# Free scatters, another quarter order, and a tile's evacuation split in two in a chunked attention and two-layer MoE kernel

## The chip, the core and the metric

One Trainium2 chip, one of its cores. Five engines work from queues of their own, each in order: TensorE (PE, with PEld for weight loads), VectorE (DVE), ScalarE (ACT), GpSimd (POOL) and SyncE (SP, which here only issues DMAs). The metric is the device time of one execution in microseconds; lower is better.

## The reference

Three stages, one behind the other, on float32 inputs:

```python
# 1. attention in chunks of 64 positions, batch 8, heads 8, sequence 576, head size 64
scores = scale * matmul(q_c, k_c.T);  scores -= max(scores)
attn = exp(scores);  attn = attn / (sum(attn) + 1e-09)
x = matmul(attn, v_c)                       # reshaped to 4608 tokens x 512
# 2. dense layer, 512 -> 2048 -> 512
h = maximum(x @ w_in, 0);  x = (h * h) @ w_out
# 3. top-1 of 8 experts, 512 -> 1024 -> 512
logits = x @ w_gate + modality_bias[modality_id]
e_idx = argmax(logits);  gate_w = softmax(logits)[e_idx]
for e in range(8):                          # the tokens whose expert is e
    out[mask] = gate_w[mask] * (maximum(x[mask] @ w1[e], 0) @ w2[e])
```

## The kernel before

**Tiles and blocks.** The 4608 tokens are 36 tiles of 128, worked on in 9 blocks of 4 tiles, counted from 0. Numbers are split into a high and a low float16 half, and a GEMM runs three passes over them.

**The dense layer of a block.** Blocks 0 to 2 compute x @ w_in plainly (`mm1`, matmul at L792). Blocks 3 to 8 use 28 products of a Strassen-like scheme (`prod`, 12 matmuls each, L621), which write four PSUM banks (two named hh, two oo); `after` brings partial results out, scaled by `al`, a factor that hangs on the largest norm in the block. `x_norm` computes that norm with a small matmul `np` (L726) and a reduction on VectorE (L728). `square` squares the hidden values into a high half (ScalarE) and a low half (GpSimd, L663). The second GEMM, `mm2` (L810), takes the four tiles one behind the other; a tile is four quarters of 12 matmuls, a quarter is four of the 16 values of f (the slices of 128 hidden units), and tile t accumulates in bank t of the four.

**The chain of a tile behind mm2.** `x2_evac` squares and sums the result on ScalarE, forms a power-of-two scale on VectorE, and writes the high and low half `xs`. `x2_tr` has SyncE transpose `xs` by DMA into `x2t` (L830) and store it to DRAM as x2d (L831). `route_a` multiplies by the gate weights (`lp`, L838) and picks the expert on VectorE (L841 to L853). `route_b` ranks the tokens of an expert (`rp`, L858 and L859). `route_c` and `route_d` scatter token and gate weight into the DRAM table `meta` by GpSimd (L884). lp, rp and np share one PSUM buffer, `ps_r`.

**Experts.** The sorted tokens are worked on in pairs of tiles, 256 tokens each. For a pair, SyncE transposes the gathered rows (L1126), 7 products give the hidden layer (L1199), 7 more the output (L1267), and `put` scatters it to `out` (L1293). SyncE and ScalarE also issue the loads of expert weights from the DRAM copy wsp (`load_part` L1075, `early_w` L1086). The products of pair 0 (`first1`) are laid between the last two tiles' mm2, those of pair 1 follow.

**What sets the order.** The program order is written by a loop over `steps` at the end: TensorE's big pieces (`mm1`, `prod`, `mm2`, `first1`) at planned times T, and before each of them `flush`, which takes from a heap the events that are due: the attention of later tiles (`attn_events`: scores, PV products `xp`, `x_tsplit`, `x_norm`), the chain of a tile, and weight work. `COST` gives what an event loads on ScalarE and VectorE; an event that finds the engine full is put off. `need` lists what must have been issued before a piece; while it is missing, flush goes on with a later time. So what is issued there stands ahead of the piece on TensorE's queue.

```python
need += [(x2_evac, b0 - 4 + t) for t in range(4)]                                   # L1642, prod
need = [(square, su, f, a[1] % 2) for f in range(0, 4 * a[2] + 4, 2)] + ...         # L1646, mm2
for t, qq in M2 if su == 0 else [(t, qq) for t in range(nt) for qq in range(4)]:    # L1570
```

Of the kernel before, what the change touches and what calls it, by code (L numbers as in the profile page):

```python
# [28 lines left out]
EW = 0.8  # L29
READY = 2  # L30
# [3 lines left out]
def kernel(  # L34
# [778 lines left out]
    def x2_evac(i):  # L813
        j = where[i][2]
# [9 lines left out]
        a["xs"], a["ui"] = xs, ui  # L824
# [57 lines left out]
    def route_d(i):  # L882
        a = x2.pop(i)
        nc.gpsimd.indirect_dma_start(  # L884
            out=meta[:, :], out_offset=bass.IndirectOffsetOnAxis(ap=a["di"][:, 0:1].bitcast(U32), axis=0),
            in_=a["mt"], in_offset=None,
        )

    mp = {}
# [17 lines left out]
    def meta_gather(n, name):  # L907
        ri = mp["ri" + name]
        if name == "a":
            mg = pp_b[0][:n]  # L910
        else:
            mg = xtall[:n, 7168:8192].bitcast(F32)
        nc.gpsimd.indirect_dma_start(
            out=mg, out_offset=None, in_=meta.rearrange("(t r) c -> t (r c)", r=PAIR),
            in_offset=bass.IndirectOffsetOnAxis(ap=ri[:n, 0:1].bitcast(U32), axis=0),
        )
        mp["mg" + name] = mg
# [244 lines left out]
    def once(fn, *a):  # L1162
        if a[-1] < PAIRS and (fn, *a) not in gone and a[-1] in pair:
            gone.add((fn, *a))
            fn(*a)

# [124 lines left out]

    def put(t, o):
        nc.gpsimd.indirect_dma_start(  # L1293
            out=out[:, :], out_offset=bass.IndirectOffsetOnAxis(ap=t.bitcast(U32), axis=0),
            in_=o, in_offset=None, bounds_check=NT - 1, oob_is_err=False,
        )

# [5 lines left out]
        x_norm: (0.0, 0.2), x2_evac: (1.2, 1.1), route_a: (0.0, 0.9),  # L1303
# [29 lines left out]
    def flush(t, n=None, room=None, dt=None):  # L1333
# [9 lines left out]
        while ev and ev[0][0] <= t or due:  # L1343
# [27 lines left out]
            if room is not None:  # L1371
# [3 lines left out]
                if full and t - at_ < SLACK and fn not in (w_form, w_split):  # L1375
# [19 lines left out]
    def attn_events(i, a0):  # L1395
# [6 lines left out]
                (43.5, x_t34, 0), (46.0, x_norm, 0), (48.0, x_tsplit, 0),  # L1402
# [154 lines left out]
    for su, (b0, nt, sb) in enumerate(supers):  # L1557
# [12 lines left out]
        for t, qq in M2 if su == 0 else [(t, qq) for t in range(nt) for qq in range(4)]:  # L1570
# [14 lines left out]
            d = (4.0, 11.0, 16.0, 19.0, 25.0) if i < NTILE - 2 and i != SEEN - 1 else (4.0, 11.0, 16.0, 19.0, 21.0) if i < NTILE - 1 and i != SEEN - 1 else (4.0, 11.0, 16.0, 19.0, 19.2) if i < NTILE - 1 else (4.0, 8.2, 12.0, 14.0, 14.5)  # L1585
            ch = [(T, x2_evac, (i,)), (T + d[0], x2_tr, (i,)), (T + d[1], route_a, (i,)), (T + d[2], route_b, (i,)), (T + d[3], route_c, (i,)), (T + d[4], route_d, (i,))]
# [38 lines left out]
    with tc.manual_schedule():  # L1625
# [3 lines left out]
        for n, (T, fn, a) in enumerate(steps):  # L1629
# [5 lines left out]
            if fn is mm1:  # L1635
                need = [(attn_x, subs[su][0] + t) for t in range(4)]
                need += [(x2_evac, a[1])] if su == PLANNED and a[1] < 2 else []
            elif fn is prod:
# [3 lines left out]
                need += [(x2_evac, b0 - 4 + t) for t in range(4)]  # L1642
            elif fn is first1:
                need = [(x2_evac, NTILE - 4), (x2_evac, NTILE - 3)][:1 + (a[0] > 0)]
            elif su >= HALVED:
                need = [(square, su, f, a[1] % 2) for f in range(0, 4 * a[2] + 4, 2)] + [(square, su, KF - 2, 0)] * (a[1] > 0)  # L1646
            elif su:
                need = [(x2_evac, supers[su][0] + a[1] - 2)]
# [151 lines left out]
```

## Time and profile before

| what | value |
|---|---|
| median of 3 runs | 1266.74 us (1266.11 to 1266.81) |
| the profiled execution's own time | 1266.4 us |
| its span | 1264.7 us |
| TensorE busy, share of the span | 1173.8 us, 93% |
| VectorE | 917.6 us, 73% |
| ScalarE | 706.6 us, 56% |
| GpSimd | 690.6 us, 55% |
| granted TensorE clock, mean | 0.978 |

The profiled execution is the one whose rows are read; its own time is longer than the span by 1.7 us, which lies around the first and last instruction. The product stretches of blocks 3 to 8 begin at 328, 416, 511.9, 604.7, 705.5 and 792 us of the span, the experts run alone from 901 us on. Busy shares are means over the span; a single stretch can look quite different, and an engine's idle time costs something only where another waits for it.

### The profile page before, as it was taken

The numbers are of one execution on the slowest core, as the hardware profiler recorded it, in microseconds if no ns is written. First come the engines' busy times: TensorE is split into PE (matmuls) and PEld (weight loads), VectorE is DVE, ScalarE is ACT, GpSimd is POOL, SyncE is SP. The second block draws the span as 40 slices with busy tenths as digits, with TensorE's granted clock in tenths as the row PEclk, the third lists the DMA queues.
The fourth block names the chain that finished last, engine by engine and source line by source line (L and its number), as shares of the span: only waits on it lengthen the run. The fifth ranks groups of instructions, "written<-read, shape, count | busy, mean of one in ns | idle before, by whom it ended". The sixth has DMA issues, their size and how long they took to land. (4 is left out here: it accounts for less than half of the span.)

```text
span 1264.7 us, 33052 instructions
## 1 busy us (share of the span) xinstructions
PE 1173.8 (93%) x12910; PEld 833.9 (66%) x12910; DVE 917.6 (73%) x2031; ACT 706.6 (56%) x1392; POOL 690.6 (55%) x641
## 2 busy tenths in 40 slices
PE   5898999999999989899989799999579999999996
PEld 4443444444774754664855664856579999999995
DVE  6899785675696895696886894854577766776663
ACT  6887583574574574574664573633335555555552
POOL 4488374587584484474574483555144455455442
PEclk9899999999899999999999899999799999999998
DMA  9455524324425537436526444255714445733241
GB/s 375 161 161 140 119 53 80 72 51 104 102 44 151 116 80 160 103 82 159 131 70 151 96 72 122 51 186 105 146 44 97 101 93 167 212 93 88 73 102 52
DMA packets 189208, 144.46 MB, mean 114 GB/s; under 512 B 126634, under 2 KB 163534, under 8 KB 187874
## 3 DMA queue, kind: packets, MB, share of 16 engines
q1 hardware_dynamic: 180386, 117.91, 38.8%
q0 software_dynamic: 7632, 20.54, 5.3%
q10 hardware_dynamic: 1008, 3.67, 1.2%
q8 instruction: 103, 1.69, 0.6%
q14 instruction: 79, 0.65, 0.2%
HBM read 204.06 MB, written 34.48 MB: 189 GB/s over the span
## 5 line engine op out<-in xcount | busy, mean ns | idle before, releaser
L810 PEld LDWEIGHTS <-big 128*128 128x128 f16 x1728 | 164.6, 98 | 203.4 <-POOL big L663 9.1
L810 PE MATMUL oo<-big,big 128*128 128x512 f16 x1056 | 237.7, 381 | 3.4 <-POOL big L772 3.4
L1199 PEld LDWEIGHTS <-big 128*128 128x128 f16 x3192 | 192.3, 99 | 20.1 <-issue 16.0
L810 PE MATMUL hh<-big,big 128*128 128x512 f16 x672 | 150.1, 379 | 6.4 <-POOL big L663 6.1
L792 PE MATMUL hh<-xtall,big 128*128 128x512 f16 x576 | 129.3, 382 | 0.1
L1199 PE MATMUL hh<-big,big 128*128 128x128 f16 x2040 | 129.0, 220 | 0.0
L621 PEld LDWEIGHTS <-big 128*128 128x128 f16 x1152 | 112.5, 99 | 22.4 <-issue 7.4
L489 POOL TENSOR_TENSOR ee<-ee,rc 128x512 f32<-128x512 f32 x36 | 39.9, 1108 | 125.1 <-DVE rc L487 71.0
L117 DVE SCALAR_TENSOR_TENSOR stage<-raw,stage 128x256 f16<-128x256 f32 x112 | 73.6, 660 | 41.9 <-ACT stage L114 36.7
L792 PEld LDWEIGHTS <-big 128*128 128x128 f16 x576 | 55.1, 98 | 64.1 <-issue 2.0
L1267 PEld LDWEIGHTS <-xtall 128*128 128x128 f16 x840 | 79.5, 98 | 11.2 <-issue 3.1
L1293 POOL DMA_INDIRECT out_dram<-raw,tib x30 | 35.5, 1183 | 90.7 <-DVE raw L117 79.2
L311 POOL TENSOR_TENSOR raw<-raw 128x256 f32<-128x256 f32 x64 | 52.7, 823 | 55.8 <-DVE stage L117 23.8
L114 ACT ACTIVATE stage<-raw 128x256 f16<-128x256 f32 x112 | 45.3, 410 | 62.3 <-DMA wsp<-stage 35.6
L772 POOL TENSOR_TENSOR big<-sn,big 128x512 f16<-128x512 f32 x48 | 59.4, 1242 | 32.4 <-DVE sn L117 16.1
L1267 PE MATMUL oo<-big,xtall 128*128 128x256 f16 x600 | 73.5, 273 | 2.7 <-DVE raw L117 2.7
L663 POOL TENSOR_TENSOR big<-r,big 128x512 f16<-128x512 f32 x48 | 61.6, 1295 | 26.1 <-ACT big L114 24.1
L663 POOL TENSOR_TENSOR big<-sn,big 128x512 f16<-128x512 f32 x48 | 61.8, 1299 | 24.0 <-ACT big L114 23.9
L114 ACT ACTIVATE big<-hh 128x512 f32<-128x512 f32 x62 | 36.9, 595 | 64.1 <-PE hh L1199 50.9
L1160 POOL TENSOR_TENSOR big<-big 128x512 f16<-128x512 f32 x34 | 39.5, 1181 | 49.6 <-ACT big L114 49.6
L117 DVE SCALAR_TENSOR_TENSOR qkt<-qk,qkt 128x1024 f16<-128x1024 f32 x32 | 47.2, 1475 | 17.3 <-ACT qkt L114 16.8
L884 POOL DMA_INDIRECT meta<-mt,di x36 | 42.2, 1172 | 22.5 <-issue 10.2
(384 smaller groups left out, 2690.3 us busy)
## 6 DMA issues: line engine op xcount, KB each, us to landing
big<-wsp SPq DMA_DIRECT2D x111, 1024.0 KB
big<-wsp SPq DMA_DIRECT2D x37, 512.0 KB
qk<-in_qk_dram SPq DMA_DIRECT2D x34, 512.0 KB
wsp<-stage SPq DMA_DIRECT2D x224, 64.0 KB
x2d<-xs SPq DMA_DIRECT2D x36, 256.0 KB
vv<-in_v_dram SPq DMA_DIRECT2D x34, 256.0 KB
big<-in_w_in_dram SPq DMA_DIRECT2D x16, 512.0 KB
raw<-in_w_out_dram SPq DMA_DIRECT2D x16, 512.0 KB
```

Of the source, the lines that this page charges most:

```text
L114: nc.scalar.activation(out=out, in_=in_, func=func, **kw)
L117: nc.vector.scalar_tensor_tensor(out=out, in0=in0, scalar=s, in1=in1, op0=op0, op1=op1, **kw)
L311: nc.gpsimd.tensor_tensor(out=quad(out_), in0=quad(in0), in1=quad(in1), op=op)
L489: eng.tensor_tensor(out=ee, in0=ee, in1=rc.unsqueeze(2).to_broadcast([128, H, 64]), op=ALU.mult)
L621: nc.tensor.matmul(ps[:, f * 256:f * 256 + 256], lhsT=block(k, la, kk, 2 * n + f), rhs=xa(lb, kk), start=k in (1, 5, 2, 4) and f + m + kk ...
L663: nc.gpsimd.tensor_tensor(out=lo, in0=c, in1=hi, op=ALU.subtract)
L772: nc.gpsimd.tensor_tensor(out=lo, in0=q32.rearrange("p (f n) -> p f n", f=nf), in1=hi, op=ALU.subtract)
L792: nc.tensor.matmul(hp[:, q_ * n:(q_ + 1) * n], lhsT=wi[:, la, kk, f * 128:f * 128 + 128], rhs=x[:, lb, kk, :], start=i == 0, stop=i == 3 * ...
L810: nc.tensor.matmul(ps, lhsT=g[:, la, f, c:c + 128], rhs=wo[:, lb, f, :], start=f == 0 and n == 0, stop=f == KF - 1 and n == 2)
L884: nc.gpsimd.indirect_dma_start(out=meta[:, :], out_offset=bass.IndirectOffsetOnAxis(ap=a["di"][:, 0:1].bitcast(U32), axis=0), in_=a["mt"], ...
L1199: nc.tensor.matmul(ps[:, f * 128:f * 128 + 128], lhsT=WB[0][:, n, la, kk, f * 128:f * 128 + 128], rhs=xa(lb, kk), start=first and f + m + ...
L1267: nc.tensor.matmul(ps, lhsT=hb[:, la, f * 128:f * 128 + 128], rhs=WB[1][:, n, lb, f, :], start=first and f + m == 0, stop=True, skip_group ...
```

## The change

**Scatters.** The scatters to `out` (`put`) and to `meta` (`route_d`) are declared free of each other (`free_of`), since each writes rows of its own; the gather of `meta` gets a dependency on every scatter ahead of it.

**Quarter order.** In blocks 3 to 8, tile 0 takes its mm2 quarters in the order 0, 2, 1, 3, and a quarter asks only for the squares of its own four f, where before it asked for those of all quarters up to it.

**Evacuation in two events.** `x2_evac` keeps the square, the sum and the scale; the new `x2_scale`, due XS = 1.5 us later, writes the two halves and `ui`. Both have a COST of their own, and neither is put off because an engine is full. The later steps of the chain are planned at 11.5, 18, 21 and 26 us behind mm2 instead of 11, 16, 19 and 25.

**Banks one by one.** A block's first four products (n = 0, k = 1, 5, 2, 4), which start the four banks, each ask for `x2_scale` of the one tile that holds their bank, where before every product asked for the evacuation of all four. In `attn_events`, x_norm is due at 54.0 instead of 46.0, behind x_tsplit.

**Pair 0.** Its products now also ask for x_sum of pair 0.

```diff
-        s, isv = scale_bits(ss, [128, 1], "ts")
+        a["xs"], a["sc"] = xs, scale_bits(ss, [128, 1], "ts")
+    def x2_scale(i):
+        j = where[i][2]
+        a = x2[i]
+        xs, (s, isv) = a["xs"], a["sc"]
         act(xs[:, 0], a["ps"], scale=s[:, 0:1])
         stt(xs[:, 1], a["ps"], s[:, 0:1], xs[:, 0], ALU.mult, ALU.subtract)
...
     def route_d(i):
-        nc.gpsimd.indirect_dma_start(
+        ins = nc.gpsimd.indirect_dma_start(
...
+        free_of(ins, "meta")
+        scattered.append(ins)
...
+        for x in scattered:
+            tc.add_manual_dep(ins.ins, x.ins.name, mybir.DependencyInfo(mybir.DependencyClass.Sync, mybir.DependencyReason.DATA))
...
+    def free_of(ins, group):
+        tc.declare_no_dep(ins.ins, group=group, reason="rows of their own")
+        tc.add_to_no_dep_group(group, ins.ins)
...
     def put(t, o):
+        free_of(ins, "out")
...
-        x_norm: (0.0, 0.2), x2_evac: (1.2, 1.1), route_a: (0.0, 0.9),
+        x_norm: (0.0, 0.2), x2_evac: (0.7, 0.4), x2_scale: (0.6, 0.8), route_a: (0.0, 0.9),
...
-                if full and t - at_ < SLACK and fn not in (w_form, w_split):
+                if full and t - at_ < SLACK and fn not in (w_form, w_split, x2_evac, x2_scale):
...
-                (43.5, x_t34, 0), (46.0, x_norm, 0), (48.0, x_tsplit, 0),
+                (43.5, x_t34, 0), (48.0, x_tsplit, 0), (54.0, x_norm, 0),
...
-        for t, qq in M2 if su == 0 else [(t, qq) for t in range(nt) for qq in range(4)]:
+        for t, qq in M2 if su == 0 else [(t, qq) for t in range(nt) for qq in ((0, 2, 1, 3) if su >= HALVED and t == 0 else range(4))]:
...
-            ch = [(T, x2_evac, (i,)), (T + d[0], x2_tr, (i,)), (T + d[1], route_a, (i,)), ...
+            ch = [(T, x2_evac, (i,)), (T + XS, x2_scale, (i,)), (T + d[0], x2_tr, (i,)), (T + d[1], route_a, (i,)), ...
...
-                need += [(x2_evac, b0 - 4 + t) for t in range(4)]
+                need += [(x2_scale, b0 - 4 + (1, 5, 2, 4).index(a[2]))] if a[1] == 0 and a[2] in (1, 5, 2, 4) else []
             elif fn is first1:
-                need = [(x2_evac, NTILE - 4), (x2_evac, NTILE - 3)][:1 + (a[0] > 0)]
+                need = [(x_sum, 0)] + [(x2_scale, NTILE - 4), (x2_scale, NTILE - 3)][:1 + (a[0] > 0)]
             elif su >= HALVED:
-                need = [(square, su, f, a[1] % 2) for f in range(0, 4 * a[2] + 4, 2)] + [(square, su, KF - 2, 0)] * (a[1] > 0)
+                need = [(square, su, f, a[1] % 2) for f in range(4 * a[2], 4 * a[2] + 4, 2)] + [(square, su, KF - 2, 0)] * (a[1] > 0)
```

**Where instructions move.** First TensorE's queue at the seam of blocks 6 and 7 (701 us in the trace before), from the last matmuls of mm2 (oo_117 is its fourth bank) to the first product of block 7, which writes hh_114; lp and rp are routing matmuls, xp is PV, np the norm. Before:

```order
L810 MATMUL oo_117<-big_88,big_89 128x512
...
L838 MATMUL lp<-wgs,x2t 128x16
...
L858 MATMUL rp<-run,ones_h 128x8
...
L859 MATMUL rp<-oh,tri_h 128x8
...
L538 MATMUL xp<-pt_105,vs_99 64x64
...
L838 MATMUL lp<-wgs,x2t 128x16
...
L621 MATMUL hh_114<-xtall,big_87 128x256
```

After (lines after L811 are those of the changed file):

```order
L539 MATMUL xp<-pt_105,vs_99 64x64
...
L727 MATMUL np<-xn_8996,ones_f 128x4
...
L811 MATMUL oo_117<-big_88,big_89 128x512
...
L622 MATMUL hh_114<-xtall,big_87 128x256
...
L622 MATMUL oo_117<-raw,big_87 128x256
```

The two lp groups, the rp pair and xp no longer stand between mm2 and the first product: xp and np stand ahead of mm2's last quarter, and routing comes later, between products.

The same place at the seam of blocks 2 and 3 (324 us before), changed kernel only:

```order
L811 MATMUL oo_117<-big_88,big_89 128x512
...
L539 MATMUL xp<-pt_105,vs_99 64x64
...
L727 MATMUL np<-xn_3314,ones_f 128x4
...
L863 MATMUL rp<-run,ones_h 128x8
...
L864 MATMUL rp<-oh,tri_h 128x8
...
L622 MATMUL hh_114<-xtall,big_87 128x256
```

Here np and the rp pair moved to the place directly ahead of the first product, and the two lp groups that stood there before are gone from it.

Second, SyncE's queue at the first pairs (from 874.88 us in the trace before), from the two transposes of pair 2 (big_89) over two weight loads (big_87) to the transpose and store of the last tile; names in brackets are the semaphores that a row waits for, and DMAHW0 to DMAHW7 are the slots that the loads and transposes of SyncE and ScalarE use in turn. Before:

```order
L1126 DMA_TRANSPOSE big_89<-big_89 128x8x128 [waits DMASW6_49,DMAHW3_49,PE_49,Pool_49]
L1126 DMA_TRANSPOSE big_89<-big_89 128x8x128 [waits DMASW7_49,PE_49,Pool_49]
...
L1075 DMA big_87<-wsp 128x2048 [waits DMAHW3_49,PE_49]
...
L1075 DMA big_87<-wsp 128x4096 [waits DMAHW4_49,PE_49]
L830 DMA_TRANSPOSE x2t<-xs 128x8x128 [waits DMAHW7_49,DMAHW6_49,DVE_49]
L831 DMA x2d<-xs 128x1024 [waits DMAHW7_49]
```

After:

```order
L1136 DMA_TRANSPOSE big_89<-big_89 128x8x128 [waits DMASW6_49,DMAHW3_49,PE_49,Pool_49]
L1136 DMA_TRANSPOSE big_89<-big_89 128x8x128 [waits DMASW7_49,DMAHW5_49,PE_49,Pool_49]
...
L1085 DMA big_87<-wsp 128x2048 [waits DMAHW3_49,PE_49]
...
L1085 DMA big_87<-wsp 128x4096 [waits DMAHW5_49,PE_49]
L835 DMA_TRANSPOSE x2t<-xs 128x8x128 [waits DMAHW7_49,DMAHW6_49,DVE_49]
L836 DMA x2d<-xs 128x1024 [waits DMAHW7_49]
```

The rows keep their order, but the second weight load now waits for slot DMAHW5 instead of DMAHW4. On ScalarE's queue at the same place, the last weight load of pair 0 (big_88) stands among the evacuations. Before:

```order
L1086 DMA big_88<-wsp 128x2048 [waits DMAHW2_49]
L114 ACTIVATE xs,ss<-oo_117 128x512 [waits DMAHW5_49,PE_49]
L114 ACTIVATE xs<-oo_117,tss 128x512 [waits DVE_49]
L114 ACTIVATE big_87<-hh_115 128x512 [waits PE_49]
L114 ACTIVATE xtall<-pt_106 128x512
...
L1086 DMA big_88<-wsp 128x2048 [waits DMAHW5_49]
L114 ACTIVATE big_87<-hh_114 128x512 [waits PE_49]
```

After:

```order
L1096 DMA big_88<-wsp 128x2048 [waits DMAHW2_49]
L115 ACTIVATE xs,ss<-oo_117 128x512 [waits PE_49]
L115 ACTIVATE big_87<-hh_115 128x512 [waits PE_49]
L115 ACTIVATE xtall<-pt_106 128x512 [waits DVE_49]
...
L1096 DMA big_88<-wsp 128x2048 [waits DMAHW4_49]
L115 ACTIVATE big_87<-hh_114 128x512 [waits PE_49]
L115 ACTIVATE ex,se<-lg,nm 128x8
L115 ACTIVATE xs<-oo_117,tss 128x512 [waits DVE_49]
```

The load asks for DMAHW4 instead of DMAHW5, and the second half of the evacuation (xs<-oo_117,tss) has moved behind it.

## Rows read from the trace of the kernel before

**Rows 1.** The page: busy time by engine; GpSimd's square group (busy, mean ns).
```profile
PE 1173.8 (93%) x12910; PEld 833.9 (66%) x12910; DVE 917.6 (73%) x2031; ACT 706.6 (56%) x1392; POOL 690.6 (55%) x641
...
L663 POOL TENSOR_TENSOR big<-r,big 128x512 f16<-128x512 f32 x48 | 61.6, 1295 | 26.1 <-ACT big L114 24.1
```

**Rows 2.** TensorE's waits: what waited for what, us, times, longest.
```profile
PE hh L1199 <- ACT big L114: 12.2, 1, 12.2
...
PE hh L810 <- POOL big L663: 6.1, 4, 2.6
PE oo L621 <- ACT r L114: 5.4, 5, 2.6
PE hh L621 <- ACT sn L114: 5.1, 4, 1.9
PE rp L858 <- DVE lg L117: 5.0, 2, 4.4
...
PE xp L538 <- DVE vs L117: 2.6, 3, 1.9
...
PE xp L538 <- ACT vs L114: 2.0, 2, 1.1
...
PE rp L859 <- DVE oh L117: 1.5, 2, 0.7
```

**Rows 3.** Busy by stretch: us, PE, PEld, DVE, ACT, POOL, clock, DMA, GB/s.
```profile
328.00:370.00 42.00, 42.00 (x509) 36.41 (x504) 36.06 (x80) 28.04 (x55) 29.03 (x27) 0.94 0.37 86
...
416.00:460.30 44.30, 41.19 (x551) 35.83 (x550) 39.41 (x88) 29.29 (x60) 26.82 (x25) 1.00 0.46 102
...
511.90:558.00 46.10, 42.30 (x528) 36.33 (x528) 37.77 (x85) 30.10 (x61) 27.98 (x26) 0.96 0.39 90
...
604.70:650.70 46.00, 41.36 (x552) 35.87 (x551) 41.23 (x91) 30.75 (x63) 25.36 (x23) 1.00 0.41 103
...
705.50:748.70 43.20, 40.57 (x452) 35.28 (x450) 40.78 (x81) 28.10 (x56) 30.29 (x28) 0.97 0.46 78
```

**Rows 4.** Timeline of TensorE, VectorE, ScalarE at 701 us: start, us, [idle before <-releaser].
```profile
701.36 0.18 PE L858 MATMUL rp<-run,ones_h 128*128 128x8 f16 x1 [4.39 <-DVE lg L117]
...
700.82 0.22 DVE L117 SCALAR_TENSOR_TENSOR lg<-lp,ui,bias_t 128x8 f32<-128x8 f32 x1
...
702.77 0.15 DVE L117 SCALAR_TENSOR_TENSOR run<-run,oh 128x8 f16<-128x8 f16 x1
...
704.22 1.23 DVE L117 SCALAR_TENSOR_TENSOR qkt<-qk,qkt 128x1024 f16<-128x1024 f32 x1 [0.26 <-ACT qkt L114]
...
706.96 0.75 DVE L117 SCALAR_TENSOR_TENSOR xs<-oo,tss,xs 128x512 f16<-128x512 f32 x1 [0.69 <-ACT xs L114]
...
703.15 1.04 ACT L114 ACTIVATE qkt<-qk 128x1024 f16<-128x1024 f32 x1
```

**Rows 5.** Timeline of the pair seam: SyncE's x2t issues, TensorE's lp, ScalarE's wait.
```profile
852.27 1.29 SPq L830 DMA_TRANSPOSE x2t<-xs  x1
...
888.10 8.69 SPq L830 DMA_TRANSPOSE x2t<-xs  x1
...
855.41 0.36 PE L838 MATMUL lp<-wgs,x2t 128*128 128x16 f16 x8
...
907.80 0.35 PE L838 MATMUL lp<-wgs,x2t 128*128 128x16 f16 x8
...
900.73 0.60 ACT L114 ACTIVATE big<-hh 128x512 f32<-128x512 f32 x1 [12.88 <-DMA big<-big]
```

**Rows 6.** Timeline of the end: VectorE's last results and GpSimd's scatters.
```profile
1250.54 0.48 DVE L117 SCALAR_TENSOR_TENSOR raw<-xq,fsb,ms 128x256 f32<-128x256 f32 x1 [2.93 <-ACT ms L114]
...
1255.78 0.88 DVE L117 SCALAR_TENSOR_TENSOR raw<-oo,fsb,ms 128x256 f32<-128x256 f32 x2 [2.12 <-PE oo L1267]
...
1251.50 1.00 POOL L1293 DMA_INDIRECT out_dram<-raw,tib  x1 [5.13 <-DVE raw L117]
...
1259.31 0.98 POOL L1293 DMA_INDIRECT out_dram<-raw,tib  x1 [3.29 <-DMA out_dram<-raw,tib]
```

More of the change, by code (lines that the diff above doesn't have):

```diff
@@ L29 @@
 EW = 0.8
+XS = 1.5
 READY = 2
@@ L813, in x2_evac @@
     def x2_evac(i):
-        j = where[i][2]
         a = x2[i]
@@ L823, in x2_evac @@
         stt(ui, isv, 1.0, blk[j]["u"], ALU.mult, ALU.mult)
-        a["xs"], a["ui"] = xs, ui
+        a["ui"] = ui
     def x2_tr(i):
@@ L887, in route_d @@
         )
+        free_of(ins, "meta")
+        scattered.append(ins)
+    scattered = []
     mp = {}
@@ L912, in meta_gather @@
             mg = xtall[:n, 7168:8192].bitcast(F32)
-        nc.gpsimd.indirect_dma_start(
+        ins = nc.gpsimd.indirect_dma_start(
             out=mg, out_offset=None, in_=meta.rearrange("(t r) c -> t (r c)", r=PAIR),
@@ L1165, in once @@
             fn(*a)
+            done.add((fn, *a))
     def banks(x, p=0):
@@ L1290, in pair_o @@
             put(t2, o2)
+    def free_of(ins, group):
+        tc.declare_no_dep(ins.ins, group=group, reason="rows of their own")
+        tc.add_to_no_dep_group(group, ins.ins)
     def put(t, o):
-        nc.gpsimd.indirect_dma_start(
+        ins = nc.gpsimd.indirect_dma_start(
             out=out[:, :], out_offset=bass.IndirectOffsetOnAxis(ap=t.bitcast(U32), axis=0),
@@ L1584 @@
                 continue
-            d = (4.0, 11.0, 16.0, 19.0, 25.0) if i < NTILE - 2 and i != SEEN - 1 else (4.0, 11.0, 16.0, 19.0, 21.0) if i < NTILE - 1 and i != SEEN - 1 else (4.0, 11.0, 16.0, 19.0, 19.2) if i < NTILE - 1 else (4.0, 8.2, 12.0, 14.0, 14.5)
-            ch = [(T, x2_evac, (i,)), (T + d[0], x2_tr, (i,)), (T + d[1], route_a, (i,)), (T + d[2], route_b, (i,)), (T + d[3], route_c, (i,)), (T + d[4], route_d, (i,))]
+            d = (4.0, 11.5, 18.0, 21.0, 26.0) if i < NTILE - 2 and i != SEEN - 1 else (4.0, 11.0, 16.0, 19.0, 21.0) if i < NTILE - 1 and i != SEEN - 1 else (4.0, 11.0, 16.0, 19.0, 19.2) if i < NTILE - 1 else (4.0, 8.2, 12.0, 14.0, 14.5)
+            ch = [(T, x2_evac, (i,)), (T + XS, x2_scale, (i,)), (T + d[0], x2_tr, (i,)), (T + d[1], route_a, (i,)), (T + d[2], route_b, (i,)), (T + d[3], route_c, (i,)), (T + d[4], route_d, (i,))]
             if i == 3:
@@ L1636 @@
                 need = [(attn_x, subs[su][0] + t) for t in range(4)]
-                need += [(x2_evac, a[1])] if su == PLANNED and a[1] < 2 else []
+                need += [(x2_scale, a[1])] if su == PLANNED and a[1] < 2 else []
             elif fn is prod:
@@ L1641 @@
                 need += [(w_split, a[1], m) for m in range(4)]
-                need += [(x2_evac, b0 - 4 + t) for t in range(4)]
+                need += [(x2_scale, b0 - 4 + (1, 5, 2, 4).index(a[2]))] if a[1] == 0 and a[2] in (1, 5, 2, 4) else []
             elif fn is first1:
-                need = [(x2_evac, NTILE - 4), (x2_evac, NTILE - 3)][:1 + (a[0] > 0)]
+                need = [(x_sum, 0)] + [(x2_scale, NTILE - 4), (x2_scale, NTILE - 3)][:1 + (a[0] > 0)]
             elif su >= HALVED:
-                need = [(square, su, f, a[1] % 2) for f in range(0, 4 * a[2] + 4, 2)] + [(square, su, KF - 2, 0)] * (a[1] > 0)
+                need = [(square, su, f, a[1] % 2) for f in range(4 * a[2], 4 * a[2] + 4, 2)] + [(square, su, KF - 2, 0)] * (a[1] > 0)
             elif su:
-                need = [(x2_evac, supers[su][0] + a[1] - 2)]
+                need = [(x2_scale, supers[su][0] + a[1] - 2)]
             else:
```

## Prediction

> **What bounds the kernel now.** I read the page first: TensorE is busy for 93% of the span, VectorE 73%, ScalarE 56%, GpSimd 55% [rows 1]. So time can come only out of TensorE's idle gaps and out of the tail behind its last matmul. The list of what TensorE waited for comes next, since it names the gaps [rows 2]. Four kinds touch the change: one wait of 12.2 us of a MoE2 product for ScalarE; 6.1 us in four waits of the second GEMM (mm2) for the squares that GpSimd subtracts; 5.0 + 2.6 + 2.0 + 1.5 = 11.1 us of small routing and PV matmuls (rp, xp) waiting for VectorE and ScalarE; and the product stretches' own waits, of which the two largest are 5.4 and 5.1 us for ScalarE. The timeline of TensorE puts the rp and xp waits, all but a few tenths, where a block's mm2 ends and the next block's products begin (seams at 328, 511 and 705 us; 4.39 us is the longest). The busy table by stretch then says what a seam's work costs elsewhere: in the product stretches VectorE is as full as TensorE, 40.78 against 40.57 of 43.2 us in the worst [rows 3]. Last, the rows at the pair seam and at the end [rows 5, 6].
>
> **The end: scatters free of each other.** Before, GpSimd's last scatter starts at 1259.31 although VectorE's last result is there at 1255.78 + 0.88 = 1256.66; it waits for the landing of the scatter ahead. The one at 1251.50 shows the lag without such a wait: 1251.50 − (1250.54 + 0.48) = 0.48 us [rows 6]. So after, it starts at about 1257.14, 2.2 us sooner; if the last two scatters share the queue and slow each other it is 1.6, if the wait for the one ahead also held the program's branch, 2.6. The meta scatters lose the same wait, but on GpSimd nothing is bound by them; the gather of meta now waits for all of them, long landed. **A = +2.2 (1.6 to 2.6).**
>
> **The pair seam.** TensorE stands still for 12.2 us while ScalarE is idle too: its row at 900.73 waited 12.88 us for the DMA transposes of pair 2, though the activation has nothing to do with them [rows 5]. In the order, ScalarE's own queue has a weight load just ahead of it that must wait for the semaphore slot (DMAHW5) which SyncE's second transpose holds. The change shifts the slots by one: that load now asks for DMAHW4, held by a load long landed, and SyncE's 128x4096 weight load asks for DMAHW5 instead. So ScalarE goes on, and SyncE stands, with the last tile's transpose x2t behind it. TensorE does the products that it did after 901.4 at once and then stands at lp of the last tile, which reads x2t. The stall is moved, and what is gained is the distance of lp from its old time, 907.80. SyncE comes free when the transposes land, 900.5 at the latest as before (900.73 less some 0.2). From there x2t takes as long as the quiet case shows, 855.41 − 852.27 = 3.1 us: lp at 903.6, +4.2; with 1.1 us more if VectorE, which in the old case had two additions ahead of the last tile's logits, is free: +5.3. The far end is the time that the very x2t took to be issued here behind the others, 8.69 us [rows 5]: 909.2, −1.4. I take lp at 905, nearer to the quiet row, since the transposes that stood in its way have landed by then: **B = +3 (−1.4 to +5.3).**
> The Trainium skill ("DMA: Bandwidth & Descriptors", section "Queues, rings and completion order") has each DMA engine go round between the queues that have work, a packet at a time, so a load that ScalarE's queue now issues 12 us sooner would take turns with SyncE's transposes and make them land later. No row of this trace shows the two side by side; by that rule B falls towards its lower end, which the range holds anyway.
>
> **The seams of two blocks.** Before, no product starts until all four tiles of the block ahead are evacuated and all routing that fell due in that time has been issued; TensorE's queue at 701 us holds lp, rp, rp, xp, lp in a row and runs in order, so it waits out VectorE's chain between lp and rp [rows 4]. After, each of the first four products asks only for its own bank, the queue has the first product straight behind mm2 at that seam, and rp stands between products. The 11.1 us [rows 2] can go. New is that the norm's reduction (np) and, at two seams, the rp pair behind it stand directly ahead of the first product, since x_norm is put 8 us later: lp, rp and np share one buffer, so rp waits until VectorE has reduced np, which stands behind a split of the next tile's q and k: 1.04 us on ScalarE and 1.23 on VectorE [rows 4]. That is 2.27 us at each of two seams, 4.5. Bounds: nothing gained, because each product then waits for the later scale (0), and all of it (11.1). **C = +6.6.**
>
> **The squares.** mm2's first tile waits four times, 6.1 us, for the lo halves of the squares [rows 2], each 1.295 us on GpSimd [rows 1]. The need is now per quarter and the order 0, 2, 1, 3, so the first of the last two squares (f = 6) has one more quarter to arrive; the very last one (f = 14) is needed at the same place as before, and where GpSimd is simply late, the wait moves there whole. Two of the four blocks have one wait each (1.14 and 1.22 in the timeline), which one quarter of mm2 covers: 2.4. In the first of them the order has one subtraction fewer ahead of the last square. Up to 6.1 goes if that holds in all; below nothing if two operations of 1.295 more stand there in another block, −2.6. **D = +3.**
>
> **What the products pay.** The work taken off the seams falls into the product stretches. By the order, the stretches of five of the six blocks change by one tile's routing on VectorE (four have one more, one less: +3 in all), and in each the last tile's second half of the evacuation comes in. One routing takes VectorE from 700.82 to 702.92, 2.1 us; the half is a 0.75 us subtraction [rows 4]: 3 x 2.1 + 6 x 0.75 = 10.8 us. The five long stretches shown leave VectorE 5.9 + 4.9 + 8.3 + 4.8 + 2.4 = 26.3 us idle [rows 3], so it could all fit (0); yet TensorE already loses over 10 us there to ScalarE and VectorE [rows 2], so it may all count (−10.8). Half of it: **E = −5.** The finer COST numbers move nothing else that the trace prices, and the first 141 us have the same order on TensorE; the rest of the first three blocks I put at 0 (−2 to +2).
>
> **Sum.** 2.2 + 3 + 6.6 + 3 − 5 = 9.8. The profiled execution took 1266.4 us, 1.7 of it outside the span of 1264.7, which stays: 1256.6. The median is 0.34 above that execution, so 1256.9, said as 1257.
>
> **Rivals.**
> 1. SyncE's new wait takes the place of ScalarE's whole: lp waits for x2t as long as the products waited for ScalarE, B = 0. For it: the 8.69 us row, and the same transposes in front. Against it: the products between run during the stall. 1260.
> 2. The product stretches take back what the seams and squares give (C + D + E = 0): for it, VectorE at 94% in the stretch from 705.5 [rows 3]; against it, 8.3 us of idle VectorE at 511.9. Left are A and B: 1267 − 5.2 = 1261.5.
> 3. Slower: the scale of the new block (al) hangs on np, and np now comes at the end of mm2 behind the split. Every snapshot of the first products waits for al, and VectorE, full, never catches up: C = 0, D = 0, E = −10.8, A + B = 5.2, net 5.6 slower: 1272. It decides for slower from the point where the products lose 5.2 more than the seams and squares give. For it: the 94%; against it: in the other stretches VectorE has a tenth or more free.
> 4. All gaps close: 2.6 + 5.3 + 11.1 + 6.1 and E = 0 give 25 us: 1242. Against it: gaps on an in-order queue rarely all vanish.
> 5. It doesn't do what it says: the slots on the chip bind elsewhere and the new order only renames the waits, leaving A: 1264.5.
>
> **How the numbers follow.** Chances: forecast 0.42, rival 1 0.16, rival 2 0.14, rival 3 0.14, rival 4 0.08, rival 5 0.06. A measurement of this kernel can tell about 0.2%, 2.5 us. Faster: 0.42 + 0.16 + 0.08 and two thirds of rival 2 = 0.75; same: the rest of rival 2 and rival 5 = 0.11; slower 0.14. The forecast's own range, with C, D and E each off by a few us, is 1250 to 1264. To leave out no more than two in ten it reaches into half of rival 4 and to the point of no change: 1246 to 1267.
>
> **What would show it.** A: the last scatter starts within 0.6 us of VectorE's last result. B: no wait of a product for ScalarE of 12 us; instead lp of the last tile waits for x2t, and comes before 907 on the old scale. C: rp and xp no longer on the list with 11 us; instead rp waits for VectorE's np reduction, about 2.3 us at two seams. D: the 6.1 us fall to 3 or less, what is left behind quarter 1. E: the waits of L621's products (by then L622) for ScalarE and VectorE grow by about 5 us. The prediction is wrong in its main step if products wait 10 us more, or if the first snapshot of each block waits for al.

## The result and the profile after

The changed kernel is slower: ratio to the kernel before 1.0086, 95% interval 1.0065 to 1.0107. Over the 16 runs of each on the same chips the medians are 1274.07 us after and 1263.06 before (its first three runs had given 1266.74), so 11 us more where 9.8 less was forecast. Repeated runs of one kernel spread over more than 10 us and chips differ, so below each kernel's time is given, and compared, as a ratio to the kernel before that ran beside it. The profiled execution took 1274.31 us, 1272.5 of it in the span.

Where it goes, by the first product of each block, the end of mm2 and the span, in us of the profiled executions (e4, e6 and e7 are explained below):

| kernel | block 3 | 4 | 5 | 6 | 7 | 8 | mm2 ends | span |
|---|---|---|---|---|---|---|---|---|
| before | 328.3 | 416.1 | 511.9 | 604.7 | 705.6 | 792.0 | 883.8 | 1264.7 |
| changed | 326.4 | 416.0 | 516.2 | 609.6 | 708.5 | 798.1 | 898.8 | 1272.5 |
| e4 | 323.3 | 411.1 | 508.3 | 603.5 | 697.5 | 792.6 | 886.5 | 1264.1 |
| e6 | 324.1 | 412.1 | 501.3 | 599.4 | 695.0 | 790.8 | 893.1 | 1262.6 |
| e7 | 323.6 | 416.4 | 511.8 | 601.3 | 706.1 | 798.6 | 900.9 | 1274.2 |

The changed kernel is 6.1 us late where block 8 begins and 15.0 us late where mm2 ends; from there to the end it takes 7.2 us less than the kernel before (373.7 for 380.9).

TensorE's waits in the changed kernel (what waited <- for what: us, times, longest), to be held against [rows 2]:

```profile
PE hh L811 <- POOL big L664: 10.6, 3, 4.9
PE lp L843 <- DMA x2t<-xs: 10.2, 1, 10.2
PE hh L622 <- ACT sn L115: 8.4, 5, 3.6
...
PE s_all L458 <- DVE ee L471: 5.8, 2, 5.6
...
PE tp L940 <- DVE ee L932: 5.1, 1, 5.1
PE rp L863 <- DVE xn L729: 4.6, 2, 2.7
...
PE oo L622 <- ACT r L115: 3.4, 3, 2.3
```

The 11.1 us of rp and xp are gone but for a few tenths, as the change means it. In their place stand rp waiting for xn (4.6), products waiting for ScalarE's snapshots sn (8.4 where 5.1 stood), scores waiting for VectorE's subtraction (5.8), more waiting for squares (10.6 for 6.1) and a wait of tp, the transposes in the map of the early pairs (5.1). The pair seam's 12.2 us behind ScalarE have become 10.2 us of lp behind x2t.

The busy table of the changed kernel in five of its product stretches (blocks 3 to 7), and the 15 us behind the tp wait (us, PE, PEld, DVE, ACT, POOL, clock, DMA, GB/s), answering to [rows 3]:

```profile
326.40:370.00 43.60, 41.51 (x502) 35.59 (x502) 36.98 (x83) 28.41 (x54) 23.66 (x21) 0.96 0.25 66
416.00:466.20 50.20, 40.25 (x502) 35.37 (x501) 41.75 (x86) 34.16 (x69) 31.55 (x29) 0.96 0.42 105
516.20:560.90 44.70, 41.88 (x502) 35.80 (x502) 39.08 (x85) 29.67 (x60) 24.98 (x24) 0.96 0.38 93
609.60:656.60 47.00, 42.48 (x502) 36.27 (x502) 38.46 (x90) 33.04 (x67) 24.02 (x23) 0.93 0.40 98
708.50:747.30 38.80, 38.80 (x455) 34.69 (x454) 32.97 (x76) 31.40 (x66) 23.69 (x22) 1.00 0.42 98
...
851.00:866.00 15.00, 15.00 (x61) 6.39 (x61) 3.19 (x18) 1.38 (x3) 6.12 (x7) 0.86 0.69 163
```

VectorE is not the bound of these stretches on average: 41.75 of 50.2 us in the longest. Not every stretch got longer: block 7's takes 38.8 us, without one idle moment of TensorE, where 43.2 stood before; but its mm2 then waits 4.91 us for squares. The longest, block 4's, holds the largest wait of scores:

```profile
465.37 0.86 PE L458 MATMUL s_all<-qkt 64*64 64x64 f16 x48 [5.64 <-DVE ee L471]
```

The last row of the table shows what came behind a stall: after the 5.1 us of tp the granted clock averages 0.86, so part of these 15 us ran at the lower of the two levels (1.2 GHz, 0.5), and 60 matmuls of mm2 took 15.18 us, where 72 took 15.91 before: 60 x (253 − 221 ns) = 1.9 us more.

**Two seams.** The timeline of the changed kernel at the seam of blocks 5 and 6 (start, us, engine, operation, [idle before <- releaser]), TensorE, then ScalarE, then VectorE:

```profile
609.39 0.39 PE L727 MATMUL np<-xn,ones_f 128*128 128x4 f32 x2
609.63 1.47 PE L622 MATMUL hh<-xtall,big 128*128 128x256 f16 x12
...
617.34 1.87 PE L622 MATMUL hh<-xtall,vs 128*128 128x256 f16 x8 [3.62 <-ACT sn L115]
...
612.10 0.42 ACT L115 ACTIVATE stage<-raw 128x256 f16<-128x256 f32 x1 [7.35 <-DMA wsp<-stage]
...
616.61 1.26 ACT L115 ACTIVATE sn<-hh,bls 128x512 f32<-128x512 f32 x2 [1.74 <-DVE bli L124]
...
612.55 0.42 DVE L118 SCALAR_TENSOR_TENSOR stage<-raw,stage 128x256 f16<-128x256 f32 x1 [4.35 <-ACT stage L115]
...
614.59 1.23 DVE L118 SCALAR_TENSOR_TENSOR qkt<-qk,qkt 128x1024 f16<-128x1024 f32 x1 [0.54 <-ACT qkt L115]
615.73 0.15 DVE L729 TENSOR_REDUCE xn<-np 128x1 f32<-128x4 f32 x1
```

np is there at 609.8, and the first product starts at once, so the seam itself has no wait. But the reduction of np runs only at 615.73: ahead of it on VectorE stand its own half of a `stage` and the qkt split, and both wait for ScalarE's half (VectorE is idle for 4.35 us at the first); ScalarE has stood 7.35 us at an activation into `stage`, whose buffer a DMA store of weights (wsp<-stage) had not yet left. So al comes at 616.6, the first snapshot with it, and the fourth product, which reuses the first bank, waits 3.62 us. Of these only 1.74 are al's: so long ScalarE stood idle for it in front of the snapshot. The rest is ScalarE's own lateness behind the store.

The seam of blocks 3 and 4 keeps the two apart. There the fourth product waits 1.58 us for the snapshot, but the reduction had been made at 413.61, before the first product (416.02); it is ScalarE that stood, again at `stage`:

```profile
413.61 0.16 DVE L729 TENSOR_REDUCE xn<-np 128x1 f32<-128x4 f32 x1 [0.16 <-PE np L727]
...
420.85 0.42 ACT L115 ACTIVATE stage<-raw 128x256 f16<-128x256 f32 x1 [3.53 <-issue]
421.18 1.25 ACT L115 ACTIVATE sn<-hh,bls 128x512 f32<-128x512 f32 x2
```

At the other four seams no snapshot waited for al. The kernel with the norm early (e4, below) has nearly the same stop of ScalarE at the seam of blocks 5 and 6, and it costs nothing there:

```profile
603.45 1.47 PE L622 MATMUL hh<-xtall,big 128*128 128x256 f16 x12
...
598.47 0.11 DVE L729 TENSOR_REDUCE xn<-np 128x1 f32<-128x4 f32 x1
...
602.69 0.42 ACT L115 ACTIVATE stage<-raw 128x256 f16<-128x256 f32 x1 [6.24 <-DMA wsp<-stage]
...
604.96 0.69 ACT L115 ACTIVATE sn<-hh,bls 128x512 f32<-128x512 f32 x1
```

There the reduction was through before ScalarE went on, and the snapshot starts as the first product's matmuls end (1.47 us from 603.45). But the stop also ended before the first product, and in the changed kernel 2.5 us behind its start, so this pair alone does not say what al cost.

### The profile page after: what moved, and what is told of

Same layout as the page of the kernel before. It is cut to its first block, busy times and chain, and to the rows that moved or that the text cites. A ratio compares the mean times of both kernels' runs of the same rounds, so it can differ in the third digit from the quotient of the medians.

```text
span 1272.5 us, 33064 instructions
## 1 busy us (share of the span) xinstructions
PE 1177.0 (92%) x12910; PEld 829.7 (65%) x12910; DVE 924.4 (73%) x2031; ACT 706.0 (55%) x1392; POOL 688.7 (54%) x641
## 5 line engine op out<-in xcount | busy, mean ns | idle before, releaser
L811 PEld LDWEIGHTS <-big 128*128 128x128 f16 x1728 | 165.5, 99 | 211.1 <-issue 13.0
L811 PE MATMUL oo<-big,big 128*128 128x512 f16 x1056 | 238.4, 381 | 3.4 <-POOL big L773 3.4
L811 PE MATMUL hh<-big,big 128*128 128x512 f16 x672 | 156.8, 392 | 12.2 <-POOL big L664 10.6
L1210 PE MATMUL s_all<-big,big 128*128 128x128 f16 x816 | 51.1, 219 | 1.1 <-ACT ms L115 1.1
```

The costliest lines, as they stand in the source:

```text
L811: nc.tensor.matmul(ps, lhsT=g[:, la, f, c:c + 128], rhs=wo[:, lb, f, :], start=f == 0 and n == 0, stop=f == KF - 1 and n == 2)
L1210: nc.tensor.matmul(ps[:, f * 128:f * 128 + 128], lhsT=WB[0][:, n, la, kk, f * 128:f * 128 + 128], rhs=xa(lb, kk), start=first and f + m + ...
```

## Experiments

Ratios are to the kernel before, run beside. "Place of np" is the count of a block's 192 mm2 matmuls that stand ahead of the norm's matmul in the order, for blocks 3 to 7; by the traces it is 84 to 144 before and 180 to 192 after.

| run | what | place of np | ratio (95%) |
|---|---|---|---|
| | changed kernel | 180 to 192 | 1.0086 (1.0065 to 1.0107) |
| e1 | before, out scatters free | 84 to 144 | 0.9993 (0.9967 to 1.0019) |
| e2 | before, quarter order | 84 to 144 | 1.0033 (1.0013 to 1.0054) |
| e3 | after, all four tiles needed | 132 to 156 | 1.0120 (1.0086 to 1.0154) |
| e4 | after, norm early | 156 to 168 | 0.9988 (0.9964 to 1.0012) |
| e5 | before, norm late | 156 to 168 | 1.0014 (1.0002 to 1.0026) |
| e6 | after, norm late, not behind x_tsplit | 108 to 180 | 1.0017 (0.9999 to 1.0035) |
| e7 | after, norm at 48.1 behind x_tsplit | 156 to 192 | 1.0074 (1.0046 to 1.0103) |
| e8 | e4 and pair 2's transposes later | 156 to 168 | 0.9915 (0.9894 to 0.9936) |
| e9 | e1 and pair 2's transposes later | 84 to 144 | 0.9897 (0.9875 to 0.9918) |
| e10 | e4 and all four tiles needed | 84 to 132 | 0.9972 (0.9955 to 0.9990) |
| e11 | e4 and old quarter order | 156 to 168 | 0.9926 (0.9899 to 0.9952) |
| e12 | e9 and norm late | 156 to 168 | 0.9893 (0.9870 to 0.9916) |
| e13 | after, old quarter order | 180 to 192 | 1.0055 (1.0039 to 1.0072) |
| e14 | e11 and pair 2's transposes later | 156 to 168 | 0.9898 (0.9872 to 0.9925) |
| e15 | after, pair 2's transposes later | 180 to 192 | 0.9994 (0.9977 to 1.0010) |

**e1, the scatters to out alone.** The lines of `free_of` and of `put` from the diff, in the kernel before.

> The kernel before, with only the scatters to out declared free of each other (the meta scatters keep their chain). Theory of the prediction: only the tail changes, 2.2 us off (1.6 to 2.6), ratio 0.9983. Rival, from the changed kernel's tail: the last scatter starts 2.4 us sooner, but runs beside the one ahead and takes longer, so that VectorE's last result to the end of the span goes from 8.04 to about 7.3 us: 0.8 us off, ratio 0.9994. Both: the last scatter starts within 0.6 us of VectorE's last result, and nothing else in the order moves.

Its end, VectorE and GpSimd:

```profile
1257.35 0.88 DVE L117 SCALAR_TENSOR_TENSOR raw<-oo,fsb,ms 128x256 f32<-128x256 f32 x2 [2.12 <-PE oo L1267]
...
1255.50 0.98 POOL L1297 DMA_INDIRECT out_dram<-raw,tib  x1 [3.56 <-DVE raw L117]
1258.50 0.98 POOL L1297 DMA_INDIRECT out_dram<-raw,tib  x1 [2.01 <-DVEq L1730]
```

The last scatter starts 0.27 us after VectorE's last result (1258.23); before it was 2.65. But from its start to the end of the span (1265.7) now go 7.2 us, where 5.4 went. The rival holds: from VectorE's result to the end go 7.47 us where 8.04 went, 0.6 us less, which the ratio can't tell from nothing.

**e2, the quarter order alone.**

```diff
-        for t, qq in M2 if su == 0 else [(t, qq) for t in range(nt) for qq in range(4)]:
+        ... for qq in ((0, 2, 1, 3) if su >= HALVED and t == 0 else range(4))]:
-                need = [(square, su, f, a[1] % 2) for f in range(0, 4 * a[2] + 4, 2)] + ...
+                need = [(square, su, f, a[1] % 2) for f in range(4 * a[2], 4 * a[2] + 4, 2)] + ...
```

> The kernel before, with only the quarter order 0, 2, 1, 3 of tile 0 and the need for a quarter's own squares. Theory of the prediction (D): the waits of mm2's first tile for GpSimd's squares fall from 6.1 us to 3 or less, time 3 us down. Rival: the order of quarters itself makes mm2 start ahead of GpSimd, and these waits rise to about 10 us as in the changed kernel (10.6), time 4 us up. Third: the waits are GpSimd's lateness, which this leaves as it is: 5 to 7 us of waits, no change in time.

TensorE's waits for squares with the quarter order alone:

```profile
PE hh L810 <- POOL big L663: 6.5, 4, 3.8
```

The two waits of 2.58 and 1.17 us in block 4 have become one of 3.75: the last square comes when it comes, and the third expectation holds for the waits. The time is 0.33% up all the same, which that expectation did not have.

**e3, all four tiles needed again.** In the changed kernel:

```diff
-                need += [(x2_scale, b0 - 4 + (1, 5, 2, 4).index(a[2]))] if a[1] == 0 and a[2] in (1, 5, 2, 4) else []
+                need += [(x2_scale, b0 - 4 + t) for t in range(4)]
```

> The changed kernel, with every product again asking for all four tiles of the block ahead (their second half of the evacuation); all else as changed. Theory 1: the loss is the seam's. The old need made the order loop run on in planned time until the evacuations were there, and so pulled the routing, the norm and the maps ahead of plan; without it they come at their planned time, late for what hangs on them. Then this kernel gets back most of the 11 us (1263 to 1267), the stall of 5.1 us of tp (the map of the early pairs) goes, and the seam waits for rp and xp come back (5 to 11 us). Rival: the loss is the later norm or the GpSimd squares and not the seam: 1271 to 1276, the tp stall stays.

Theory 1, that the new need is what costs, falls: the kernel gets nothing back (1.0120 where the changed kernel has 1.0086; the intervals overlap). Its largest wait:

```profile
PE rp L863 <- DVE lg L118: 25.5, 5, 11.1
```

With the chain's later delays, lp and rp of the last tiles stand ahead of the first product and wait out VectorE, in five of six blocks. (np stands earlier here, as the program order is written: the old need makes flush run on in planned time ahead of the products. So e3 undoes part of the norm's place as well, and the two are told apart only by e4 to e7.)

**e4, the norm early.** In the changed kernel:

```diff
-                (43.5, x_t34, 0), (48.0, x_tsplit, 0), (54.0, x_norm, 0),
+                (43.5, x_t34, 0), (46.0, x_norm, 0), (48.0, x_tsplit, 0),
```

> The changed kernel, with x_norm due at 46.0 ahead of x_tsplit again; all else as changed. Theory 2: the norm put 8 us later is what costs: rp waits for np's reduction (4.6 us at two seams) and the second user of the first bank waits for a snapshot that needs al (1.6 + 3.6 us), together 9.8; with the norm early all of it goes, 1264 to 1267. Theory 1 (the seam's need costs): these waits go, but the chain's lateness stays (tp 5.1 us, squares some 10 us): 1268 to 1272. Rival: the norm's place does nothing, 1274.

The whole loss goes with this one line. Its waits:

```profile
PE lp L843 <- DMA x2t<-xs: 17.3, 3, 15.7
...
PE s_all L458 <- DVE ee L471: 7.4, 3, 3.1
...
PE hh L811 <- POOL big L664: 4.1, 3, 3.0
...
PE hh L622 <- ACT sn L115: 1.9, 3, 0.9
```

No rp waits for xn, sn is at 1.9 (8.4), the squares at 4.1 (10.6), tp at 0.5 (5.1). Other waits rose, lp most (17.3 for 10.2), so that the list as a whole is only some 4 us shorter. The 9.8 us expected from three direct waits lie near the 1.0%, 12 us, that came, but not as a reckoning: of the waits for snapshots in them, the 1.6 us were not the norm's at all, and of the 3.6 only 1.74 were (the two seams above). With the pair seam's wait out of both kernels (e8 and e15, below) the same line is worth 0.8%, 10 us.

**e5 to e7, which of its two sides costs: the later due time, or the place behind x_tsplit.** x_tsplit of a block is held until the block ahead has issued its last product, and the chain is in order, so whatever is queued behind it comes in mm2 at the earliest. e5 is e4's edit the other way round, in the kernel before; e6 and e7 edit the changed kernel:

```diff
# e6
-                (43.5, x_t34, 0), (48.0, x_tsplit, 0), (54.0, x_norm, 0),
+                (43.5, x_t34, 0), (48.0, x_tsplit, 0),
...
+        at_time(a0 + 54.0, x_norm, i)
# e7
-                (43.5, x_t34, 0), (48.0, x_tsplit, 0), (54.0, x_norm, 0),
+                (43.5, x_t34, 0), (48.0, x_tsplit, 0), (48.1, x_norm, 0),
```

> The kernel before, with only x_norm moved to 54.0 behind x_tsplit. In the order np then stands behind 156 to 168 of a block's 192 mm2 matmuls (before 84 to 156; in the changed kernel 180 to 192; in the changed kernel with the norm early 156 to 168). Theory 1: what costs is np at the very end of mm2, so that al and the shared buffer come too late for the first products; here np is a quarter or two early enough: 1260 to 1266, no waits of rp for xn, the first snapshots not late. Rival: x_norm's later due time costs by itself, whatever stands around it: 1270 to 1275.

> The changed kernel, with x_norm due at 54.0 still but as an event of its own, not queued behind x_tsplit. np then stands behind 108 to 180 matmuls of mm2. Theory 1 (the place at the end of mm2 costs, and it comes from x_tsplit, which is held until the block's products are through): 1260 to 1265, about as with the norm early. Rival (the 8 us later due time costs): 1270 to 1275.

> The changed kernel, with x_norm due at 48.1, at once behind x_tsplit. np stands behind 180 to 192 matmuls of mm2 in four of the five later blocks, though due 6 us sooner than in the changed kernel. Theory 1: as slow as the changed kernel, 1270 to 1276, with rp waiting for xn and ScalarE's first snapshot late. Rival (the due time costs): 1260 to 1266.

In their times all three came as the theory of the place has them: e7, due 6 us sooner, is as slow as the changed kernel; e6, due as late, is not. (In e5 the maps slip past pair 0, whose first products read their rows before they are summed; the work done is the same, and e12, where they ask for x_sum, is no slower than e9.)

By the stretches the place is only half of it. Where block 8 begins, e7 is as late as the changed kernel (798.6 and 798.1 us), and e6 and e4 are where the kernel before is (790.8 and 792.6; 792.0): that part hangs on the place. But block 8 itself, up to the end of mm2, takes 100.7 us in the changed kernel and about as long in e5, e6 and e7 (102.5, 102.3, 102.3), against 93.9 in e4 and 91.8 before. It holds the tp wait, which stands in e5 and e6 too (5.4 and 5.2 us), so it comes with the later norm wherever np stands. tp waits there for a gather of `meta` (GpSimd), just behind which SyncE issues four weight loads; GpSimd, SyncE and VectorE of the changed kernel, then GpSimd and VectorE of e4:

```profile
839.60 0.95 POOL L921 DMA_INDIRECT pp<-meta,ria  x1 [4.92 <-DVE ria L1005]
...
840.27 2.80 SPq L1085 DMA_DIRECT2D big<-wsp  x4
...
849.58 0.86 DVE L932 COPY ee<-pp 4x512 f32<-4x512 f32 x1 [5.71 <-issue]
```

```profile
832.15 0.95 POOL L921 DMA_INDIRECT pp<-meta,ria  x1 [2.72 <-DVE ria L1005]
...
837.73 0.62 DVE L932 COPY ee<-pp 4x512 f32<-4x512 f32 x1
```

From the issue of the gather to its first reader went 10.0 us in the changed kernel and as long in e5 and e6, where the loads begin 0.5 and 0.6 us behind it; 5.6 in e4, where three of the four are issued ahead of it, and 4.0 before, where they come 5.6 us behind it. No run moves these loads alone, so that they make the difference is argued and not shown. e5 and e6 are not slow in the end because they reach block 8 sooner and because their stall at the pair seam is shorter (7.3 and 7.2 us, against 12.2 before and 15.7 in e4).

In e7 it is np itself that waits, since lp and rp hold the shared buffer just ahead of it, and the first product waits behind it:

```profile
PE s_all L458 <- DVE ee L471: 9.0, 2, 5.1
PE tp L940 <- DVE ee L932: 5.7, 1, 5.7
...
PE np L727 <- DVE dj L118: 4.2, 2, 3.7
```

**e8, e9, e15: pair 2's transposes later.** The same edit with the norm early, in the kernel before (with e1), and in the changed kernel:

```diff
-                    at_time(T + 6.5, once, x_tr, 2)
+                    at_time(T + 17.0, once, x_tr, 2)
```

> The changed kernel with the norm early, and in addition the two transposes of pair 2 issued behind the last tile's x2t, x2d and the third weight load instead of 15 us ahead of them. Theory: these transposes share the DMA engines with seven weight loads of 512 KB, take 25 us to land, and block whatever load has their slot; moved, neither ScalarE nor SyncE stands, lp of the last tile no longer waits 15.7 us for x2t, and most of that comes off: 1248 to 1253 (ratio 0.990 to 0.993). Rival: the transposes land late at the new place too, the sums of pair 2 on VectorE wait, and the time stays: 1259 to 1264.

> The kernel before with the scatters to out free, and the two transposes of pair 2 issued behind the last tile's x2t, x2d and the third weight load. Theory: the 12.2 us in which the first pair's products wait for ScalarE are those transposes and nothing else; without them in flight the wait is under 1 us: 1250 to 1253, ratio 0.990 to 0.993, as with the norm early. Rival: it is worth it only where SyncE stands (the changed kernel's slots), and ScalarE's wait stays or another takes its place: 1258 to 1263.

> The changed kernel, norm late, with only the transposes of pair 2 moved. lp of the last tile waits 10.2 us for x2t there, behind SyncE's blocked load. If that wait is those transposes alone, it goes whole: ratio 0.998 to 1.001. If the changed kernel's later routing would have held lp anyway, half stays: 1.003 to 1.006.

SyncE at the pair seam in the changed kernel, with TensorE's lp, and then SyncE in e9:

```profile
889.90 5.04 SPq L1136 DMA_TRANSPOSE big<-big  x2
901.10 14.15 SPq L1085 DMA_DIRECT2D big<-wsp  x2
915.37 1.25 SPq L835 DMA_TRANSPOSE x2t<-xs  x1
...
918.47 0.38 PE L843 MATMUL lp<-wgs,x2t 128*128 128x16 f16 x8 [10.20 <-DMA x2t<-xs]
```

```profile
888.27 2.54 SPq L1075 DMA_DIRECT2D big<-wsp  x2
890.93 1.25 SPq L830 DMA_TRANSPOSE x2t<-xs  x1
...
893.59 7.30 SPq L1126 DMA_TRANSPOSE big<-big  x4
```

In the changed kernel the loads hold SyncE for 14.15 us, until the transposes issued at 889.90 have landed; in e9 they go out at once, x2t with them, and no wait of 12 or 10 us is left on TensorE's list. The theory holds in all three: 1.0% off the kernel before, 0.9% off the changed kernel, 0.7% with the norm early. e8 against e15 also gives the price of the norm without this wait in either: 0.9915 and 0.9994.

**e10, e11, e13: seam and quarter order again, with the norm out of the way.** e10 is e3's edit and e11 e2's undone, both with the norm early; e13 is the quarter order undone in the changed kernel.

> The changed kernel with the norm early, and with every product asking for all four tiles again. Theory 1: asking bank by bank is worth the waits of rp at the seams (25 us with the late norm, 11 in the kernel before), less what comes back as waits inside the products: slower than with the norm early alone by 4 to 12 us, 1266 to 1274. Rival: the seam's gain is paid back whole, so that undoing it costs nothing: 1259 to 1264.

> The changed kernel with the norm early, and with tile 0 in the quarter order 0, 1, 2, 3 and the old need of squares. Theory: the order of quarters moves a wait and takes none away, and costs 4 us alone, so undoing it gains 0 to 4 us on the norm early: 1258 to 1262. Rival (the prediction's D): it is worth 3 us, 1264 to 1266.

> The changed kernel with tile 0's quarters in the order 0, 1, 2, 3 again; the norm stays late. If the quarter order is part of the loss of the changed kernel, this takes 3 to 6 us off 1.0086 (ratio 1.004 to 1.006), and the waits for squares fall from 10.6 us. If the loss is the norm's place alone (np stands behind the same 180 to 192 matmuls), the ratio stays at 1.007 to 1.010 and the waits for squares stay near 10 us.

e10 against e4 (0.9972, 0.9988): asking bank by bank is worth nothing that can be told, though e10's waits of rp are 14.5 us and e4's 4.5. Its rival holds. (Where block 8 begins e4 is 3.2 us ahead, 792.6 and 795.8, but its lp then waits 15.7 us at the pair seam for 9.7; the pair without that wait was not run.) The new quarter order is the worse one each time: by 0.3% alone (the interval clear of 1), 0.6% with the norm early (intervals apart), 0.3% in the changed kernel and 0.2% with the transposes moved (intervals overlap). It is not by the squares: in e13 these waits are 10.4 us, in the changed kernel 10.6. What else it does is open.

**e12 and e14, the parts put together.** e12: e9, norm late, pair 0 asking for its x_sum. e14: e11 and the transposes.

> The kernel before with the scatters to out free, x_norm at 54.0 behind x_tsplit, pair 0's products asking for its x_sum, and the transposes of pair 2 moved. With the norm late alone block 8's products began 8 us sooner than before (784 against 792) and gave it back later in tp (5.4 us) and the pair seam (7.3). Theory: the transposes' share adds to it: 1248 to 1254. Rival: pair 0's x_sum is late by the whole of what was gained, since the maps hang on the last seen tile's routing, and the first products of pair 0 wait for it: 1256 to 1262.

> The changed kernel with the norm early, the old quarter order, and the transposes of pair 2 moved: what the runs so far point to. If the parts add (0.9926 with the first two, about 0.01 for the transposes), ratio 0.981 to 0.985, 1240 to 1246 on a chip where the kernel before takes 1264. If the old order's gain was chance, the ratio is that of the norm early and the transposes alone, 0.990 to 0.993.

Both beat the two kernels, and neither beats e9: the parts don't add. e12's block 8 begins its products at 786 us (792 before), and 5.4 us of it go to tp:

```profile
838.84 0.59 PE L930 MATMUL tp<-id_f,ee 4*128 4x4 f32 x4 [5.42 <-DVE ee L922]
```

e14 came out at 0.990 where adding gave 0.981 to 0.985. No version is better beyond its interval than the simplest, e9: the kernel before with two transposes moved and free scatters.

## Why the prediction was wrong

**The step that failed** is C, the seams, at +6.6: 11.1 us of waits that go, less the price of the late norm, "rp waits until VectorE has reduced np, which stands behind a split of the next tile's q and k ... That is 2.27 us at each of two seams, 4.5." Both terms were mis-sized. The late norm was priced by one wait, and for that wait the 4.5 was right (rp 2.72 + 1.86 = 4.6 us at two seams). Undoing it gives back 10 to 12 us (e4; e8 against e15). About half of that is lost up to the first product of block 8 and hangs on np's place at the end of mm2: rp's 4.6 us and al's 1.74 of ScalarE at one seam have about its size, though other waits rose and fell beside them. The other half is lost in block 8, where the map's gather came beside four weight loads, tp waited 5.1 us and the matmuls behind it took 1.9 more; the prediction had no term for it. And the 11.1 us of waits, taken away, were worth nothing that the time shows (e10 against e4).

**Rival 3** named late al, with 1272 us and a chance of 0.14. It had the direction, and the order already showed np directly ahead of the first product at two seams; but its mechanism came at one seam of six and for 1.74 us, not at every first snapshot, and not because VectorE was full on average: VectorE was 83% busy in the slowest stretch. At that seam it stood idle behind ScalarE, and ScalarE behind a DMA store, for which the prediction, pricing the operations ahead of the reduction, had nothing. That 1272 lies close to the 1274.07 measured is luck: it was 5.6 us slower than 1266.4, and 11 slower came.

**C without the late norm** (+11.1 before its price): e10 against e4 says about nothing. The waits of rp and xp do go, but in e4 the scores wait 7.4 us for VectorE and rp 4.5 for run. That is rival 2, for the seams.

**D** (+3) is nothing in the waits (6.5 for 6.1 alone; 10.6 for 10.4) and a loss in time. The trace before could have said so: three of its four waits (1.17, 1.14 and 1.22 us, in blocks 4, 5 and 6) stand behind 44 of the first tile's 48 matmuls, at the very last square, which is needed at the same place in either order. Only the 2.58 us, at f = 6, could move, and they moved there whole. The two short waits that the spare quarter was to cover stand unchanged in e2 (1.14 and 1.21).

**A** (+2.2) was right in its step and wrong in its sum: the scatter starts 2.4 us sooner, but takes 1.8 longer beside the one ahead (e1); I had let 0.6 for that.

**B** (+3, −1.4 to +5.3) came as described: SyncE in ScalarE's place, x2t behind it, lp 3.1 us after SyncE comes free (915.37 to 918.47). From the issue of pair 2's transposes to lp went 907.80 − 874.88 = 32.9 us before and 28.6 after, 4.3 gained; by TensorE's own waits it is 2.0 (12.2 and 10.2). The Trainium skill's rule that I weighed there ("DMA: Bandwidth & Descriptors", section "Queues, rings and completion order": engines take turns between queues) would have had them land later with the seventh load ahead. From issue to landing they took 25.4 us after (889.90 to 915.25), at most 25.9 before (874.88 to 900.73, [rows 5]), beside six of the seven loads, but 30.6 in e4 (877.74 to 908.38, below), with that load ahead as well, so the traces don't settle it. e4's SyncE at the same place:

```profile
877.74 5.53 SPq L1136 DMA_TRANSPOSE big<-big  x2
893.86 14.52 SPq L1085 DMA_DIRECT2D big<-wsp  x2
```

That is where e4's lp waits its 15.7 us. The prediction left out something larger than B: both waits are those two transposes, which need not be issued there. e9 took 1.0% for one number.

**E** (−5) did not come where it was looked for: the products' waits for ScalarE's r fell from 5.4 to 3.4 us. It came at the scores, which now wait 5.64 us for VectorE in block 4's stretch (465.37, above); VectorE worked without a pause from 451.89 until then, 3.4 us of it on a tile's routing.

**The terms as the runs have them**, an estimate from the ratios and waits above: A 0.6, B 2 to 4, C with E −10 to −12, D −4, together 9 to 13 us slower. 11 were measured; 9.8 the other way were forecast.

## What to carry to other kernels

When a small operation is moved later, list everything that hangs on its result, not only the next instruction on the bounding engine, and price its queue by what the engines ahead of it wait for (at one seam here a DMA store two engines away held it for 6 us), not by how long their operations take. A list of waits that an in-order engine no longer has is not yet a gain: here 11 us of them vanished and the time did not fall. Compare where each stage begins, too: it shows which half of a loss an experiment gave back. Where one wait of 12 us is put down to a DMA that the waiting work doesn't need, move that DMA first.

## What the runs showed of the hardware

- A DMA transpose of 128x8x128 had its reader start 3.1 us after it was issued while no weights moved (x2t: 915.37 to lp at 918.47); two of them took 25 to 31 us beside the weight loads, in three kernels.
- A gather of 4 rows had its reader start 10.0 us after it was issued where four weight loads followed from 0.7 us behind it on, 5.6 where three of them were issued ahead of it, and 4.0 where none came for 5.6 us.
- A scatter started while the one ahead is in flight ends little sooner: 7.2 us from start to the end of the span against 5.4.
- Behind a stall of 5.1 us the granted clock averaged 0.86 over 15 us, and 60 matmuls took 1.9 us more than at the pace of the kernel before.
